# A pass width for each expert, and in the last stage a PSUM bank for the exponential with another order on ScalarE

## The chip, the cores and the metric

The kernel runs on one core of one Trainium2 chip. The metric is the device time of one launch in microseconds (us). A core has TensorE (PE, with its weight loads shown apart as PEld), VectorE (DVE), ScalarE (ACT), GpSimd (POOL) and SyncE (SP, which here only issues DMAs). Each engine works through its own instructions in the order in which they stand, and waits at an instruction until what it needs is there.

## The reference

Three parts follow each other. The first is attention with a window of 32 and 32 global positions (4 batches, 8 heads, 544 positions). The second routes each of the 2176 rows of the first to one of 8 experts. The third is a feed-forward layer with a rational function.

```python
# part 2, for each expert e (x: 2176 x 512, w1[e]: 512 x 1024, w2[e]: 1024 x 512)
mask = e_idx == e                      # e_idx = argmax(x @ w_gate)
h = np.maximum(x[mask] @ w1[e], 0.0)
out[mask] = gate_w[mask, None] * eom[mask, e, None] * (h @ w2[e])

# part 3 (w_in: 512 x 2048, w_out: 2048 x 512)
h = x @ w_in
P = a[0] + a[1] * h + a[2] * h * h + a[3] * h * h * h
Q = 1.0 + np.abs(b[0]) * np.abs(h) + np.abs(b[1]) * h * h
y = (P / (Q + 1e-06)) @ w_out
```

How many rows an expert gets depends on the data. The inputs are drawn with a fixed seed; the reference's own router gives on them, for experts 0 to 7, the counts 422, 331, 253, 249, 220, 149, 434 and 118.

## The kernel before, in words

Matrices are kept as a pair of a rounded high part and a low part, and each product is made of three matmuls (high by high, high by low, low by high), so the instruction counts are three times what one would expect.

**Experts.** Tokens are gathered by expert into an `x` tile (`xs` for expert 0, then `xa` and `x2c` in turn), columns being tokens. `wide` (line 898) is the pass without a branch: it works on the first 256 columns of an expert (`BASE`), and for expert 0 on the first 296 (`FIRST`). It takes 8 steps of 12 matmuls for the first product (line 914, into `ph`) and, two steps behind (`LAG`), 8 steps of 12 matmuls for the second (line 926, into four accumulators `acc`): 192 matmuls whose width is the number of columns. Between them ACT makes the high part of the hidden layer (`hT`, line 919) and DVE the low part (line 920). The `hT` tiles are used in turn: five of them at 256 columns, four at 296.

Tokens beyond the pass are handled in blocks of 128 columns by `single` (line 852), each behind a branch on the expert's count, in `beyond` (line 1014): the outer branch is `cnt > 256` (line 1022), the inner one `cnt > 384` (line 1024). `single` has 24 matmuls of 512 columns (line 872), transposes (lines 860 and 891) and 48 matmuls of 256 columns (line 882), and POOL stores its result (line 846). The blocks of expert e run inside the pass of expert e+1, after that one's first step (`AFTER`); while they run, the background work of the pass (weights split into high and low parts, lines 693 and 697, gathers, loads of `x`) stands still. Expert 6's columns 256 to 511 are prepared ahead, in expert 5's pass (`READY`).

**Last stage** (`moe2`, line 1213). 17 blocks of 128 tokens in five chunks of 4, 3, 4, 3 and 3 blocks (`CH`), each of 16 steps, so steps 0 to 79. In a step PE makes `h` (line 1162, 12 matmuls, 512 or 384 columns wide), the elementwise chain makes the rational function in high and low parts `gh` and `gl`, and PE multiplies these with `w_out` (line 1305, 3 matmuls of 512 columns for each block of the chunk). From step 48 on the second product runs four steps behind the first (`SK + 1`), and `gh` and `gl` have four places each, all in one tile. The elementwise chain of a step (`elem`, line 1255) in its order on each engine:

- ACT: `ab` (1265), `u` (1266), `q` (1267), then `gh` of the step before (1279), the logarithm `r0` (1282), the exponential `r` (1284)
- POOL: `q` times `ab` (1268), which needs ACT's `q`; the logarithm needs its result
- DVE: two operations on `u` (1271, 1272), `gl` of the step before (1280), then after the exponential `q` (1288), `r` (1291), `u` (1295); the next step's `gh` needs that last `u`

In chunk 0 the exponential is written to a PSUM bank (`bank_r`), in the others in place in SBUF (`r0`). In `last` (line 1327) the final three steps' second products are made block by block, and each block is copied out of PSUM (1335, 1337, 1338) and scattered to its rows by POOL (1314).

Of the kernel before, what the change touches and what calls it, by code (L numbers as in the profile page):

```python
# [24 lines left out]
E = 8  # L25
# [12 lines left out]
ACT_EXP_LN = 6  # L38
STEP = 6
NB = 2  # L40
BASE, MOST, FIRST, LAG = 256, 512, 296, 2
NX, HINT = 4, 8
READY, LATER = (6,), (5, 7)
SA, S0, S1 = "v", "a", "a"


# [21 lines left out]
TR = (1, 1), (2, 2)  # L68
HB = 4
AY = 14, 11, 2  # L70
LASTS = 3
LEAD = 2
YQ = lambda nc: nc.scalar
AQ = lambda nc: nc.gpsimd
# [27 lines left out]
class Build:  # L102
# [715 lines left out]
    def experts(self, st, first, gate):  # L818
# [5 lines left out]
        self.xgs += [xg.tile([128, DM + 1], F32, name=f"xg{n}") for n in range(2, NX)]  # L824
        for x in self.xgs[2:]:
            nc.gpsimd.memset(x, 0.0)
        yt = P("yp").tile([128, 4, FIRST], F32, name="yt")
        hp = P("hp")
        PP = lambda name, bufs: st.enter_context(tc.tile_pool(name=name, bufs=bufs, space=PSUM))
        ps_h = self.ps_h = self.ctx.enter_context(tc.tile_pool(name="ps_h", bufs=2, space=PSUM))  # L830
# [3 lines left out]
        ps_t = lambda: pools[next(turn) % len(pools)]  # L834
        col = lambda e, j: self.idx[:, NBLK * e + j:NBLK * e + j + 1]
        X = lambda e: self.xs if e == 0 else self.xa if e % 2 else self.x2c
        hT = [hp.tile([128, 2, FIRST if n < 4 else BASE], F32R, name=f"hT{n}") for n in range(NH)]
        hr = [hp.tile([128, 512], F32, name=f"hr{n}") for n in range(2)]
        PAIRS = ((0, 0), (0, 1), (1, 0))

        ORDER = [(k, 0, b) for k in range(4) for b in range(2)] + [(k, 1, 0) for k in range(4)]
        off = [0]

        def store(e, j, n, y, q):

            q.dma_start(out=self.ybuf[:, :, bass.ds(off[e] + 128 * j, n)], in_=y)

        def store_rest(y):

            nc.sync.dma_start(out=self.ybuf[:, :, FIRST:FIRST + 128], in_=y)  # L850

        def single(e, j, x, at=0, put=None, W=None, parts=2):

            W = W or self.slot[e % 2]
            hk = lambda a, k: hT[AFTER + k // 2][:, a, 128 * (k % 2):128 * (k % 2) + 128]

            def transp(n):
                pt = ps_t().tile([128, 4, 128], F32, tag="pt", name="pt")
                for c in range(4):
                    nc.tensor.transpose(pt[:, c], hr[n][:, 128 * c:128 * c + 128], self.ident)  # L860
                for a in range(2):
                    o = [hT[AFTER + 2 * n + a][:, i, 0:256] for i in range(2)]
                    self.split_t(*o, pt[:, 2 * a:2 * a + 2].rearrange("p c t -> p (c t)"))

            def hook(n, k):
                if (n, k) in TR:
                    transp(n - 1)

            for n in range(2):
                ph = ps_a.tile([128, 512], F32, tag=f"acc{n + 1}", name=f"acc{n + 1}")  # L870
                for i, (k, a, b) in enumerate(ORDER):
                    nc.tensor.matmul(ph, lhsT=x[:, a, k, at:at + 128], rhs=W[:, b, 2 * k + n, :], start=(i == 0), stop=(i == 11))
                    if i % 3 == 2:
                        hook(n, i // 3)
                nc.scalar.activation(hr[n], ph, AF.Relu)
            w = 512 // parts
            py = [ps_a.tile([128, 512], F32, tag=f"acc{m}", name=f"acc{m}")[:, 0:w] for m in (0, 3)[:parts]]
            for ks in [(k,) for k in range(6)] + [(6, 7)]:
                for m in range(parts):
                    for k in ks:  # L880
                        for i, (a, b) in enumerate(PAIRS):
                            nc.tensor.matmul(py[m], lhsT=hk(a, k), rhs=W[:, b, 8 + k, w * m:w * m + w],
                                             start=(k == 0 and i == 0), stop=(k == 7 and i == 2))
                for k in ks:
                    hook(2, k)
            y, yc = hr[0], hr[1].rearrange("p (c t) -> p c t", c=4)
            nc.scalar.copy(y[:, :256], py[0][:, 0:256])
            nc.vector.tensor_copy(y[:, 256:], py[-1][:, w - 256:w])
            pt = ps_t().tile([128, 4, 128], F32, tag="pt", name="pt")
            for c in range(4):  # L890
                nc.tensor.transpose(pt[:, c], y[:, 128 * c:128 * c + 128], self.ident)
            nc.scalar.copy(yc, pt)
            put(yc) if put else store(e, j, 128, yc, AQ(nc))

        def mark(label, hint):
            tc.mark_branch_hint_location(label, hint, [mybir.EngineType.PE])

        def wide(e, j, n, x, bg, last=True, acc=None, before=None):

            W = self.slot[e % 2]  # L900
            nh = NH if n <= BASE else 4
            rest, bg = bg, iter(()) if before else bg
            acc = [ps_a.tile([128, 512], F32, tag=f"acc{m}", name=f"acc{m}") for m in range(4)] if acc is None else acc
            for s in range(8 + LAG):
                if s == HINT and e:
                    mark(f"rest{e}", cnt[e] > BASE)
                if s == AFTER and before:
                    before()
                    bg = rest
                if s < 8:  # L910
                    ph = ps_h.tile([128, 512], F32, tag="ph", name="ph")[:, :n]
                    c = 128 * (s % 4)
                    for i, (k, a, b) in enumerate(ORDER):
                        nc.tensor.matmul(ph, lhsT=W[:, b, 2 * k + s // 4, c:c + 128], rhs=x[:, a, k, :n],
                                         start=(i == 0), stop=(i == 11))
                        if i % 6 == 5:
                            next(bg, None)
                    hi, lo = (hT[s % nh][:, a, :n] for a in range(2))
                    nc.scalar.activation(hi, ph, AF.Relu)
                    nc.vector.scalar_tensor_tensor(out=lo, in0=ph, scalar=0.0, in1=hi.bitcast(F32),  # L920
                                                   op0=ALU.max, op1=ALU.subtract)
                if s >= LAG:
                    f = s - LAG
                    for m in range(4):
                        for i, (a, b) in enumerate(PAIRS):
                            nc.tensor.matmul(acc[m][:, :n], lhsT=W[:, b, 8 + f, 128 * m:128 * m + 128],  # L926
                                             rhs=hT[f % nh][:, a, :n], start=(f == 0 and i == 0), stop=(f == 7 and i == 2))
                        if m % 2:
                            next(bg, None)
            def end():  # L930
                for m in range(4):
# [1 line left out]
                k = min(NBLK, 128 - NBLK * e)  # L933
                YQ(nc).dma_start(out=self.toks[bass.ds(off[e], 128 * k), :].rearrange("(j p) o -> j (p o)", p=128),
                                 in_=self.idxT[NBLK * e:NBLK * e + k])
                store(e, j, n, yt[:, :, :n], YQ(nc))

            if last:
                end()
# [47 lines left out]
        def more(e, j, end):  # L987

            with tc.For_i(j, end, 1) as i:
                tok = self.ixo[:, 1:2].bitcast(F32)  # L990
                nc.gpsimd.tensor_copy(tok, self.idx[:, bass.ds(i + NBLK * e, 1)])
                self.prep(NX - 1, X(e), ps_t(), 0, after=lambda: fetch(e, i + 1))
                single(e, i, X(e))
                AQ(nc).dma_start(out=self.toks[bass.ds(off[e] + 128 * i, 128), :], in_=tok,
                                 allow_slow_non_contiguous=True)

# [10 lines left out]
        def expert(e, early=lambda: ()):  # L1007

            plan = PLANW if e < E - 1 else PLANW7
            more_ = blocks(e + 1 if e + 1 in READY else e, (2, 3)) if e + 1 in READY or e not in READY + LATER else []  # L1010
            wide(e, 0, BASE, X(e), weave(todo(e, plan, None, blocks(e + 1, (0, 1)) + more_, more_ + blocks(e + 2, (0, 1))),
                                         iter(early())), before=(lambda: beyond(e - 1)) if e > 1 else second)

        def beyond(e):
            def rest_block(b, parts):
                if e in LATER:
                    self.gather(b, col(e, b))
                    self.scale(b, 128, S1)
                if e not in READY:
                    self.prep(b, X(e), ps_t(), 128 * b, scale=False, parts=2)  # L1020
                single(e, b, X(e), 128 * b, parts=parts)
            with tc.If(cnt[e] > BASE, label=f"rest{e}"):  # L1022
                rest_block(2, 2)
                with tc.If(cnt[e] > BASE + 128):
                    rest_block(3, 2 if e in READY else 1)

        def reload(e):

# [35 lines left out]


        acc = [ps_a.tile([128, 512], F32, tag=f"acc{m}", name=f"acc{m}") for m in range(4)]
        wide(0, 0, FIRST, self.xs, woven(), False, acc)()
        gate.close()
        pools.append(PP("ps_t2", 1))
        self.conv_init(P("cv"))  # L1070
# [3 lines left out]
        def second():  # L1074
# [5 lines left out]
            j0, end0 = (nc.s_assert_within(x, 0, NBLK) for x in (j0, end0))  # L1080
            self.conv_first()
            with tc.If(more0 > 0):
                single(0, 2, self.xs, put=store_rest)
            with tc.If(again0 > 0):
                fetch(0, j0)
                more(0, j0, end0)
# [126 lines left out]
    def moe2(self):  # L1213
        nc, tc, out = self.nc, self.tc, self.t["out"]
        with ExitStack() as st:
# [26 lines left out]
            load_y = lambda ch, i: self.load_y(chunks[ch][0] + i)  # L1242
            prep = lambda ch, i: self.x2_prep(chunks[ch][0] + i, x2[ch], i, nc.gpsimd if ch == 1 else nc.vector)
            steps = [(c, f) for c in range(len(chunks)) for f in range(16)]
            hs, gs, us, accs, out_, rows = {}, {}, {}, {}, [], []
            n_steps = len(steps)

            def gemm1(s):
# [6 lines left out]
            def elem(s):  # L1255
# [5 lines left out]
                if s < n_steps:  # L1261
# [1 line left out]
                    h = hs.pop(s)[:, :w]  # L1263
                    ab, q, u, r0 = (et[t_][s % len(et[t_])][:, :w] for t_ in ("ab", "q", "u", "r0"))
                    nc.scalar.activation(ab, h, AF.Abs)  # L1265
                    nc.scalar.activation(u, h, AF.Identity, scale=a3, bias=a2)  # L1266
                    nc.scalar.activation(q, ab, AF.Identity, scale=b1, bias=b0)  # L1267
                    nc.gpsimd.tensor_tensor(out=q, in0=q, in1=ab, op=ALU.mult)  # L1268
                    if rows:
                        rows.pop(0)()  # L1270
# [9 lines left out]
                    GL(nc, s - 1).tensor_tensor(out=g[1], in0=up, in1=g[0].bitcast(F32), op=ALU.subtract)  # L1280
                if s < n_steps:
                    nc.scalar.activation(r0, q, AF.Ln, bias=eps1)  # L1282
                    r = bank_r[:, :w] if first_ch(s) else r0
                    nc.scalar.activation(r, r0, AF.Exp, scale=-1.0)  # L1284
                if out_:
                    store(out_.pop())
# [193 lines left out]
```

## Time and profile before

| | |
|---|---|
| median of 3 runs | 797.82 us (796.57 to 799.12) |
| the profiled execution | 796.99 us, its span 795.4 us |
| PE, PEld busy share | 97%, 83% |
| DVE, ACT, POOL busy share | 73%, 67%, 46% |
| granted TensorE clock, mean | 0.997 of full speed |

The span is the time from the first to the last instruction; 1.6 us of the run lie around it. A busy share is an average over stages. PE's time is modelled from the starts of its matmuls, which overlap, so the time of a group is best read from start to start of the groups around it.

### The profile page before, as it was taken

To read this page: it belongs to the slowest core of one execution; us is meant where nothing else is said; L and a number is where in the kernel's file an instruction comes from. 1 tells how busy PE (TensorE), PEld (TensorE's weight loads), DVE (VectorE), ACT (ScalarE), POOL (GpSimd) and SP (SyncE) were. 2 spreads that over 40 slices of the span, in tenths; PEclk is the share of its full clock that TensorE was granted. 3 is DMA by queue.
4 is the path that set the end of the run, shared out by engine and by line. 5 is a ranking of instruction groups with operands and counts; after the bars stand their busy time and mean duration, and the time that the engine had idled before them with its cause. 6 is when DMAs were issued, how large, how long until landed. Compare 5 with 4: busy or idle time off the path is not lost. (4 is left out here: it accounts for less than half of the span.)

```text
span 795.4 us, 17092 instructions
## 1 busy us (share of the span) xinstructions
PE 769.5 (97%) x6144; PEld 661.9 (83%) x6145; DVE 579.6 (73%) x1426; ACT 536.7 (67%) x1206; POOL 366.5 (46%) x415
## 2 busy tenths in 40 slices
PE   8999998899999999999999999999999999999995
PEld 5767666798989999998988888888888898988983
DVE  5669788662828877771369999888888768888883
ACT  4667675563646766652668888878877767877772
POOL 4445555363617667540565877432252214323422
PEclk9999999999999999999999999999999999999998
DMA  8998993465748989892263440010010000000101
GB/s 296 306 314 283 278 304 106 138 190 191 269 137 269 323 292 339 302 310 71 94 185 111 120 108 25 28 54 27 0 55 14 0 1 28 27 0 1 41 1 40
DMA packets 52701, 112.88 MB, mean 142 GB/s; under 512 B 10786, under 2 KB 24866, under 8 KB 50552
## 3 DMA queue, kind: packets, MB, share of 16 engines
q1 hardware_dynamic: 42232, 96.39, 37.6%
q0 software_dynamic: 3888, 9.80, 3.9%
q10 hardware_dynamic: 6480, 5.39, 2.1%
q8 instruction: 57, 0.93, 0.5%
q14 instruction: 44, 0.36, 0.2%
HBM read 95.42 MB, written 19.03 MB: 144 GB/s over the span
## 5 line engine op out<-in xcount | busy, mean ns | idle before, releaser
L1268 POOL TENSOR_TENSOR q<-q,ab 128x384 f32<-128x384 f32 (+1 forms) x78 | 97.9, 1255 | 209.6 <-ACT q L1267 201.4
L1305 PE MATMUL acc<-slot,gh 128*128 128x512 f32 x528 | 165.8, 395 | 1.5 <-ACT gh L1279 1.5
L697 POOL TENSOR_TENSOR slot<-raw,slot 128x512 fp32r<-128x512 f32 x84 | 112.9, 1353 | 69.4 <-ACT slot L693 65.9
L1162 PE MATMUL ph<-x2c,slot 128*128 128x512 f32 (+1 forms) x552 | 125.1, 374 | 0.9 <-PEq L1022 0.4
L1162 PEld LDWEIGHTS ph<-x2c,slot 128*128 128x128 f32 x552 | 101.1, 187 | 19.6 <-ACTq L1134 0.7
L1305 PEld LDWEIGHTS acc<-slot,gh 128*128 128x128 f32 x528 | 98.3, 187 | 21.8 <-ACT gh L1279 1.9
L1305 PE MATMUL acc<-slot,gl 128*128 128x512 f32 x264 | 104.4, 395 | 0.0
L926 PE MATMUL acc<-hT,slot 128*128 128x256 f32 (+1 forms) x768 | 102.8, 284 | 0.0
L926 PEld LDWEIGHTS acc<-hT,slot 128*128 128x128 f32 x768 | 96.2, 189 | 0.2
L693 ACT CAST slot<-raw 128x512 fp32r<-128x512 f32 x144 | 85.4, 619 | 9.4 <-DVE yt L932 4.9
L314 POOL TENSOR_SCALAR pr<-ex,r 128x128 f32<-128x128 f32 x128 | 46.6, 376 | 57.0 <-PE sc L261 17.6
L1162 PE MATMUL ph<-xa,slot 128*128 128x384 f32 x384 | 71.8, 336 | 0.0
L1282 ACT ACTIVATE r<-q,cab 128x384 f32<-128x384 f32 (+1 forms) x78 | 51.4, 658 | 28.6 <-POOL q L1268 27.5
L1162 PEld LDWEIGHTS ph<-xa,slot 128*128 128x128 f32 x384 | 67.9, 188 | 2.7
L1288 DVE SCALAR_TENSOR_TENSOR q<-q,r 128x384 f32<-128x384 f32 (+1 forms) x64 | 38.6, 603 | 40.1 <-ACT r L1284 40.1
L1279 ACT CAST gh<-u 128x384 fp32r<-128x384 f32 (+1 forms) x78 | 43.4, 556 | 33.4 <-DVE u L1295 20.1
L697 DVE TENSOR_TENSOR slot<-raw,slot 128x512 fp32r<-128x512 f32 x60 | 50.4, 841 | 17.4 <-ACT slot L693 16.9
L296 ACT ACTIVATE ex<-sm,mx 128x128 f32<-128x128 f32 x128 | 50.3, 395 | 15.9 <-POOL pr L314 8.5
L1266 ACT ACTIVATE u<-ph,cab 128x384 f32<-128x384 f32 (+1 forms) x78 | 55.3, 708 | 7.1 <-POOL gl L1280 6.1
L1305 PEld LDWEIGHTS acc<-slot,gl 128*128 128x128 f32 x264 | 49.4, 187 | 12.3 <-DVE gl L1280 0.3
L1267 ACT ACTIVATE q<-ab,cab 128x384 f32<-128x384 f32 (+1 forms) x78 | 58.1, 745 | 0.0
L1272 DVE SCALAR_TENSOR_TENSOR u<-u,cab,ph 128x384 f32<-128x384 f32 (+1 forms) x78 | 51.9, 666 | 2.8
(232 smaller groups left out, 1486.4 us busy)
## 6 DMA issues: line engine op xcount, KB each, us to landing
raw<-in_w_dram SPq DMA_DIRECT2D x78, 512.0 KB
vw<-in_vw_dram SPq DMA_DIRECT2D x16, 1024.0 KB
r<-in_w_dram SPq DMA_DIRECT2D x18, 512.0 KB
kw<-in_kw_dram SPq DMA_DIRECT2D x16, 384.0 KB
raw<-wf SPq DMA_DIRECT2D x9, 512.0 KB
qt<-in_qT_dram SPq DMA_DIRECT2D x32, 128.0 KB
xbuf<-xrow SPq DMA_DIRECT2D x8, 512.0 KB
ybuf<-yt ACTq DMA_DIRECT2D x7, 512.0 KB
```

The source lines that it names most:

```text
L296: nc.scalar.activation(ex[:, h], src[:, h], AF.Exp, bias=mx[:, h:h + 1], scale=-1.0, accum_out=ssum[:, h:h + 1])
L314: nc.gpsimd.tensor_scalar(out=pr[:, h], in0=ex[:, h], scalar1=r[:, h:h + 1], scalar2=1.0, op0=ALU.mult, op1=ALU.mult)
L693: nc.scalar.copy(hi, r)
L697: eng.tensor_tensor(out=lo[:, c], in0=r[:, c], in1=hi[:, c].bitcast(F32), op=ALU.subtract)
L926: nc.tensor.matmul(acc[m][:, :n], lhsT=W[:, b, 8 + f, 128 * m:128 * m + 128], rhs=hT[f % nh][:, a, :n], start=(f == 0 and i == 0), stop=(f ...
L1162: self.nc.tensor.matmul(ph[:, :w], lhsT=l[a], rhs=r[b], start=(k == 0 and i == 0), stop=(k == 3 and i == 2))
L1266: nc.scalar.activation(u, h, AF.Identity, scale=a3, bias=a2)
L1267: nc.scalar.activation(q, ab, AF.Identity, scale=b1, bias=b0)
L1268: nc.gpsimd.tensor_tensor(out=q, in0=q, in1=ab, op=ALU.mult)
L1272: nc.vector.scalar_tensor_tensor(out=u, in0=u, scalar=a1, in1=h, op0=ALU.add, op1=ALU.mult)
L1282: nc.scalar.activation(r0, q, AF.Ln, bias=eps1)
L1305: nc.tensor.matmul(accs[i], lhsT=l[a], rhs=Wo[:, b, f, :], start=(f == 0 and j == 0), stop=(f == 15 and j == 2))
```

## The change

1. A table `WIDE` gives the width of the pass: 296 columns for expert 0, as before, and 308 for expert 6, the seventh; all others keep 256. Every place that assumed 256 now takes the expert's own width: the branches of `beyond`, the prefetch hint (line 906), the position of the blocks and of their stores. Expert 6's blocks so begin at columns 308 and 436, its branches are `cnt > 308` and `cnt > 436`. The `x` tile ends at column 512, so the second block would read from column 384 and store its last 76 columns.
2. The five `hT` tiles become two: one for the first place, as wide as the widest pass, and one that is cut into the other places by the pass's width. At 308 columns four places are used in turn.
3. From step 54 of the last stage on (`SPARE`) ACT makes `q` ahead of `u`, and the exponential and what follows from it (lines 1284 to 1295) go to the PSUM bank of the fourth accumulator, which the last two chunks, three blocks wide, don't use.

```diff
-BASE, MOST, FIRST, LAG = 256, 512, 296, 2
+BASE, MOST, LAG = 256, 512, 2
-READY, LATER = (6,), (5, 7)
+READY, LATER, WIDE = (6,), (5, 7), {0: 296, 6: 308}
+FIRST = WIDE[0]
-LASTS = 3
+LASTS, SPARE = 3, 54
...
-        yt = P("yp").tile([128, 4, FIRST], F32, name="yt")
+        wd = lambda e: WIDE.get(e, BASE)
+        widest = max(wd(e) for e in range(E))
+        yt = P("yp").tile([128, 4, widest], F32, name="yt")
...
-        hT = [hp.tile([128, 2, FIRST if n < 4 else BASE], F32R, name=f"hT{n}") for n in range(NH)]
+        h0, hs = (hp.tile([128, 2 * w], F32R, name=f"hT{n}") for n, w in enumerate((widest, (NH - 1) * BASE)))
+        hT = lambda k, n: (hs[:, 2 * n * (k - 1):2 * n * k] if k else h0[:, 0:2 * n]).rearrange("p (a t) -> p a t", a=2)
...
-            nh = NH if n <= BASE else 4
+            nh = min(NH, 1 + (NH - 1) * BASE // n)
...
-                    mark(f"rest{e}", cnt[e] > BASE)
+                    mark(f"rest{e}", cnt[e] > n)
...
-            wide(e, 0, BASE, X(e), weave(todo(e, plan, None, blocks(e + 1, (0, 1)) + more_, more_ + blocks(e + 2, (0, 1))),
+            wide(e, wd(e), X(e), weave(todo(e, plan, None, blocks(e + 1, (0, 1)) + more_, more_ + blocks(e + 2, (0, 1))),
...
         def beyond(e):
-            def rest_block(b, parts):
-                if e in LATER:
-                    self.gather(b, col(e, b))
-                    self.scale(b, 128, S1)
-                if e not in READY:
+            def rest_block(c, parts):
+                at = min(c, MOST - 128)
+                for b in range(-(-c // 128), (at + 127) // 128 + 1) if e not in READY else ():
+                    if e in LATER:
+                        self.gather(b, col(e, b))
+                        self.scale(b, 128, S1)
                     self.prep(b, X(e), ps_t(), 128 * b, scale=False, parts=2)
-                single(e, b, X(e), 128 * b, parts=parts)
-            with tc.If(cnt[e] > BASE, label=f"rest{e}"):
-                rest_block(2, 2)
-                with tc.If(cnt[e] > BASE + 128):
-                    rest_block(3, 2 if e in READY else 1)
+                single(e, c, X(e), at, parts=parts, skip=c - at)
+            n = wd(e)
+            with tc.If(cnt[e] > n, label=f"rest{e}"):
+                rest_block(n, 2)
+                with tc.If(cnt[e] > n + 128):
+                    rest_block(n + 128, 2 if e in READY else 1)
...
-                    nc.scalar.activation(u, h, AF.Identity, scale=a3, bias=a2)
-                    nc.scalar.activation(q, ab, AF.Identity, scale=b1, bias=b0)
+                    for o_, x_, k1, k0 in ((q, ab, b1, b0), (u, h, a3, a2))[::1 if s >= SPARE else -1]:
+                        nc.scalar.activation(o_, x_, AF.Identity, scale=k1, bias=k0)
...
-                    r = bank_r[:, :w] if first_ch(s) else r0
+                    if s == SPARE:
+                        spare.append(ps_a.tile([128, 512], F32, tag="acc3", name="acc3"))
+                    r = bank_r[:, :w] if first_ch(s) else spare[0][:, :w] if spare else r0
```

On PE, at the end of expert 6's pass, where expert 7's first step and the branch to expert 6's blocks follow, the kernel before has this (`slot_81` holds expert 6's weights, `slot_3338` expert 7's; `acc`, `hT` and `ph` are as above):

```order
L926 MATMUL acc_6653<-hT_3368,slot_81 128x256 x3
L926 MATMUL acc_6654<-hT_3368,slot_81 128x256 x3
L914 MATMUL ph<-xa,slot_3338 128x256 x12
L1022 COMPARE_AND_BRANCH
L872 MATMUL acc_7186<-slot_81,x2c 128x512 x12
```

At the same place the changed kernel has this:

```order
L930 MATMUL acc_6650<-hT_3367,slot_81 128x308 x3
L930 MATMUL acc_6651<-hT_3367,slot_81 128x308 x3
L918 MATMUL ph<-xa,slot_3338 128x256 x12
L1028 COMPARE_AND_BRANCH
L876 MATMUL acc_7183<-slot_81,x2c 128x512 x12
```

Only the width of expert 6's matmuls differs, 308 in place of 256. Their number and place are the same, expert 7's step keeps 256, and both blocks still stand in the program, behind their branches.

On ACT, near the end of the last stage, one step of the kernel before (`q` is written at line 1267, the logarithm at 1282, the exponential at 1284):

```order
L1265 ACTIVATE ab_8285<-ph 128x384
L1266 ACTIVATE u_8288<-ph,cab 128x384
L1267 ACTIVATE q_8286<-ab_8285,cab 128x384
L1279 CAST gh<-u_8289 128x384
L1282 ACTIVATE r_8290<-q_8286,cab 128x384
L1284 ACTIVATE r_8290<-r_8290 128x384
```

The same step in the changed kernel (both `u` and `q` are now of line 1273):

```order
L1271 ACTIVATE ab_8282<-ph 128x384
L1273 ACTIVATE q_8283<-ab_8282,cab 128x384
L1273 ACTIVATE u_8285<-ph,cab 128x384
L1285 CAST gh<-u_8286 128x384
L1288 ACTIVATE r_8287<-q_8283,cab 128x384
L1292 ACTIVATE acc_10362<-r_8287 128x384
```

`q` has moved ahead of `u`, and the exponential goes from the logarithm's SBUF tile to the PSUM bank `acc_10362`. The cast to `gh` keeps its place ahead of the logarithm.

## Rows read from the trace of the kernel before

**Rows 1.** The page, busy time and share of the span by engine.
```profile
PE 769.5 (97%) x6144; PEld 661.9 (83%) x6145; DVE 579.6 (73%) x1426; ACT 536.7 (67%) x1206; POOL 366.5 (46%) x415
```

**Rows 2.** Chain of work that ended last, its end: start us, length us, engine, work.
```profile
727.35 2.09 PE ph L1162 x12
729.44 2.12 PE acc L1305 x9
...
732.56 0.56 ACT u L1266
...
776.40 0.56 ACT u L1266
...
782.59 5.30 PE acc L1305 x21
```

**Rows 3.** Timeline, steps 78 and 79: start us, length us, engine, line, tiles, [idle before].
```profile
769.06 2.26 PE L1162 MATMUL ph<-x2c,slot 128*128 128x384 f32 x12
...
775.93 0.47 ACT L1265 ACTIVATE ab<-ph 128x384 f32<-128x384 f32 x1
...
776.30 0.67 ACT L1266 ACTIVATE u<-ph,cab 128x384 f32<-128x384 f32 x1
...
776.86 0.71 ACT L1267 ACTIVATE q<-ab,cab 128x384 f32<-128x384 f32 x1
...
777.64 1.18 POOL L1268 TENSOR_TENSOR q<-q,ab 128x384 f32<-128x384 f32 x1 [2.82 <-ACT q L1267]
...
778.85 0.62 ACT L1282 ACTIVATE r<-q,cab 128x384 f32<-128x384 f32 x1 [0.31 <-POOL q L1268]
...
779.50 0.53 ACT L1284 ACTIVATE r<-r 128x384 f32<-128x384 f32 x1
...
780.72 0.40 PE L1305 MATMUL acc<-slot,gl 128*128 128x512 f32 x1
...
782.03 0.51 ACT L1279 CAST gh<-u 128x384 fp32r<-128x384 f32 x1 [2.00 <-DVE u L1295]
782.57 0.56 DVE L1280 TENSOR_TENSOR gl<-u,gh 128x384 fp32r<-128x384 f32 x1 [0.63 <-ACT gh L1279]
...
782.59 0.73 PE L1305 MATMUL acc<-slot,gh 128*128 128x512 f32 x2 [1.47 <-ACT gh L1279]
```

**Rows 4.** Timeline of PE, expert 6's two blocks.
```profile
355.95 4.29 PE L872 MATMUL acc<-slot,x2c 128*128 128x512 f32 x18
...
368.93 0.44 PE L891 MATMUL pt<-ident,hr 128*128 128x128 f32 x2 [0.27 <-DVE hr L888]
369.12 4.38 PE L872 MATMUL acc<-slot,x2c 128*128 128x512 f32 x18
...
382.42 3.13 PE L914 MATMUL ph<-xa,slot 128*128 128x256 f32 x24
```

**Rows 5.** Timeline of PE, after expert 1's only block.
```profile
234.19 0.44 PE L891 MATMUL pt<-ident,hr 128*128 128x128 f32 x2 [0.27 <-DVEq L1024]
235.06 3.00 PE L914 MATMUL ph<-x2c,slot 128*128 128x256 f32 x24 [0.42 <-PEq L1024]
```

**Rows 6.** Busy time by engine, 370 to 380 us: length; PE, PEld, DVE, ACT, POOL; clock, DMA.
```profile
370.00:380.00 10.00, 10.00 (x66) 8.91 (x65) 1.70 (x4) 2.73 (x7) 0.81 (x1) 1.00 0.09 27
```

**Rows 7.** Timeline of PE in expert 6's pass, 256 columns.
```profile
340.60 1.53 PE L914 MATMUL ph<-x2c,slot 128*128 128x256 f32 x12
...
343.38 1.55 PE L914 MATMUL ph<-x2c,slot 128*128 128x256 f32 x12
```

**Rows 8.** Timeline of PE in expert 0's pass, 296 columns.
```profile
155.58 1.81 PE L926 MATMUL acc<-hT,slot 128*128 128x296 f32 x12
...
160.49 1.80 PE L914 MATMUL ph<-xs,slot 128*128 128x296 f32 x12
```

**Rows 9.** Groups by line, chunk 0 (414 to 490 us): xcount, busy us, mean ns.
```profile
L1295 DVE SCALAR_TENSOR_TENSOR u<-u,cab,ph 128x512 f32<-128x512 f32 x13 | 9.6, 739 | 0.0
```

**Rows 10.** The same line in chunk 2 (570 to 645 us).
```profile
L1295 DVE SCALAR_TENSOR_TENSOR u<-u,cab,r 128x512 f32<-128x512 f32 x15 | 11.3, 752 | 0.5
```

More of the change, by code (lines that the diff above doesn't have):

```diff
@@ L842, in experts, with store, single @@
         off = [0]
-        def store(e, j, n, y, q):
-            q.dma_start(out=self.ybuf[:, :, bass.ds(off[e] + 128 * j, n)], in_=y)
+        def store(e, c, n, y, q):
+            q.dma_start(out=self.ybuf[:, :, bass.ds(off[e] + c, n)], in_=y)
         def store_rest(y):
             nc.sync.dma_start(out=self.ybuf[:, :, FIRST:FIRST + 128], in_=y)
-        def single(e, j, x, at=0, put=None, W=None, parts=2):
+        def single(e, to, x, at=0, put=None, W=None, parts=2, skip=0):
             W = W or self.slot[e % 2]
-            hk = lambda a, k: hT[AFTER + k // 2][:, a, 128 * (k % 2):128 * (k % 2) + 128]
+            hk = lambda a, k: hT(AFTER + k // 2, BASE)[:, a, 128 * (k % 2):128 * (k % 2) + 128]
             def transp(n):
@@ L861, in transp @@
                 for a in range(2):
-                    o = [hT[AFTER + 2 * n + a][:, i, 0:256] for i in range(2)]
+                    o = [hT(AFTER + 2 * n + a, BASE)[:, i] for i in range(2)]
                     self.split_t(*o, pt[:, 2 * a:2 * a + 2].rearrange("p c t -> p (c t)"))
@@ L892, in single, with wide @@
             nc.scalar.copy(yc, pt)
-            put(yc) if put else store(e, j, 128, yc, AQ(nc))
+            put(yc) if put else store(e, to, 128 - skip, yc[:, :, skip:], AQ(nc))
         def mark(label, hint):
             tc.mark_branch_hint_location(label, hint, [mybir.EngineType.PE])
-        def wide(e, j, n, x, bg, last=True, acc=None, before=None):
+        def wide(e, n, x, bg, last=True, acc=None, before=None):
             W = self.slot[e % 2]
-            nh = NH if n <= BASE else 4
+            nh = min(NH, 1 + (NH - 1) * BASE // n)
             rest, bg = bg, iter(()) if before else bg
@@ L917, in wide @@
                             next(bg, None)
-                    hi, lo = (hT[s % nh][:, a, :n] for a in range(2))
+                    hi, lo = (hT(s % nh, n)[:, a] for a in range(2))
                     nc.scalar.activation(hi, ph, AF.Relu)
@@ L926, in wide @@
                             nc.tensor.matmul(acc[m][:, :n], lhsT=W[:, b, 8 + f, 128 * m:128 * m + 128],
-                                             rhs=hT[f % nh][:, a, :n], start=(f == 0 and i == 0), stop=(f == 7 and i == 2))
+                                             rhs=hT(f % nh, n)[:, a], start=(f == 0 and i == 0), stop=(f == 7 and i == 2))
                         if m % 2:
@@ L935, in end @@
                                  in_=self.idxT[NBLK * e:NBLK * e + k])
-                store(e, j, n, yt[:, :, :n], YQ(nc))
+                store(e, 0, n, yt[:, :, :n], YQ(nc))
             if last:
@@ L992, in more @@
                 self.prep(NX - 1, X(e), ps_t(), 0, after=lambda: fetch(e, i + 1))
-                single(e, i, X(e))
+                single(e, 128 * i, X(e))
                 AQ(nc).dma_start(out=self.toks[bass.ds(off[e] + 128 * i, 128), :], in_=tok,
@@ L1066, in experts @@
         acc = [ps_a.tile([128, 512], F32, tag=f"acc{m}", name=f"acc{m}") for m in range(4)]
-        wide(0, 0, FIRST, self.xs, woven(), False, acc)()
+        wide(0, FIRST, self.xs, woven(), False, acc)()
         gate.close()
@@ L1082, in second @@
             with tc.If(more0 > 0):
-                single(0, 2, self.xs, put=store_rest)
+                single(0, 256, self.xs, put=store_rest)
             with tc.If(again0 > 0):
@@ L1244, in moe2 @@
             steps = [(c, f) for c in range(len(chunks)) for f in range(16)]
-            hs, gs, us, accs, out_, rows = {}, {}, {}, {}, [], []
+            hs, gs, us, accs, out_, rows, spare = {}, {}, {}, {}, [], [], []
             n_steps = len(steps)
```

## Prediction

> **What bounds the kernel now.** I read the page's busy shares first: PE works 97% of the span, no other engine over 83% [rows 1]. So a change counts by what it takes from PE's own time, or from the few places where PE stands still. The chain of waits says where those are. From the start of the last stage it runs through PE alone, `ph` and `acc` in turn, up to 731.56 us; from there to 782.59 us it runs through the elementwise chain of ACT, POOL and DVE, and then through PE's last 21 matmuls [rows 2]. A step there costs PE 2.1 + 2.1 = 4.2 us. The elementwise chain, from ACT's `u` at 732.56 to the `u` of eleven steps later at 776.40, takes 43.84/11 = 3.99 us a step [rows 2]: a little less than PE's 4.2, so that once it is behind it hardly catches up.
>
> The timeline shows the bill. PE finishes its last `ph` group, begun at 769.06, and has only second products left, for which it needs each step's `gh`. Its last one before the gap starts at 780.72; at 9 matmuls in 2.1 us, 0.233 us each, the next was due at 780.95. It starts at 782.59, when step 79's `gh` is there [rows 3]. That is 1.64 us. The following 21 take 5.30 us [rows 2], where 20 x 0.233 + 0.40 = 5.07 would do (the wait for `gl`): 0.23 us more. So 1.87 us of PE's time in the tail are the elementwise chain's doing.
>
> Then the experts, on PE's timeline. Expert 6 has two blocks behind branches, from 355.95 and from 369.12, and at 382.42 expert 7's pass goes on [rows 4]. A block is 13.2 to 13.3 us in which PE hardly stops.
>
> **The wider pass.** With 308 columns in the pass, a second block is needed from 437 tokens on. The reference's router gives expert 6 434, so it goes. Removed are 382.42 - 369.12 = 13.30 us of PE. What comes in its place is a branch that is now not taken. Expert 1 shows this case: its inner branch is not taken either, and from the start of the block's last transposes to the next matmul pass 235.06 - 234.19 = 0.87 us [rows 5], against 369.12 - 368.93 = 0.19 us where the branch goes on into the second block [rows 4]. So expert 7's pass would go on at 368.93 + 0.87 = 369.80 us instead of 382.42: 12.62 us less.
>
> Added are 52 columns in each of expert 6's 192 matmuls. At 256 columns, 24 of them take 343.38 - 340.60 = 2.78 us, 115.8 ns each [rows 7]. At 296, 36 take 160.49 - 155.58 = 4.91 us, 136.4 ns [rows 8]. At 384, 12 take 2.09 us, 174 ns [rows 2]. Between the last two 308 lies 12 columns above 296, at 0.43 ns a column: 141.6 ns; on from the first two, at 0.52 ns: 142.6. I take 142: 192 x 26.2 = 5.03 us more. The bounds are the rows on both sides: 136.4 ns gives 3.96 us, 174 ns gives 11.2 us.
>
> [...]
>
> What else the wider pass moves: four `hT` places in turn instead of five, where expert 0 ran at 136.4 ns with four, so no wait is added. The `hT` tiles become parts of one tile; `gh` and `gl` are already kept so, and there the chain shows PE without a gap between steps [rows 2], so parts are told apart. ACT's and DVE's work on `hT` and the store grow by a fifth, beside PE. The stores, of 308 and at the narrow end 76 columns, are read back only in the last stage. Background work of expert 7's pass has nothing to lose by the missing block, since it stands still in one: from 370 to 380 us DVE is busy 1.70, ACT 2.73, POOL 0.81 us and the DMA engines 9% [rows 6]. It begins 12.6 us sooner, with the same pace against PE as before. Should loads be late after all, the cover is that first block, 13 us.
>
> **The last stage.** `q` ahead of `u` lets ACT start `q` when `ab` is done, 775.93 + 0.47 + 0.03 (the gap between ACT's logarithm and exponential) = 776.43 instead of 776.86: 0.43 us sooner for POOL and all behind it [rows 3]. By that chain alone a step would take 3.56 us. But ACT's cast to `gh` of the step before stands ahead of the logarithm: from the exponential's end (780.03) to the start of the cast are 2.00 us of DVE, then 0.51 the cast, 0.62 the logarithm, 0.53 the exponential and 0.03 between: 3.7 us [rows 3]. That is what a step takes then, 0.3 us under the 3.99 of before. Over the eleven steps the chain gains 3.2 us on its old place; it needs 1.6.
>
> The bank adds a freedom: the logarithm no longer waits until DVE has read `r`. Its price is DVE working on PSUM. Chunk 0 does this already: the last `u` takes 739 ns there [rows 9] and 752 ns with `r` in SBUF [rows 10]. I take zero, between a gain of 0.04 us a step (three operations of 13 ns) and nothing.
>
> [...]
>
> A limit stands behind that. `gh` has four places, so step 78's cast waits for PE to finish step 74's second product: from 769.06 + 2.10 come steps 73 and 74, done about 775.5. Step 79's logarithm is queued behind this cast on ACT. Then cast, logarithm and exponential (to 777.3), 2.00 of DVE, and step 79's `gh` is there at 779.8, `gl` 0.56 later, against 780.95 and 781.4 when PE asks. One us of room: the whole 1.87 us goes, and the end, copies and POOL's scatters, follows PE as it does now.
>
> **The sum.** -12.62 + 5.03 - 1.87 = -9.46 us. Against the profiled execution's own time, 796.99 us (a span of 795.4 and 1.6 around it), that is 787.5. This execution lies 0.83 us under the median of 797.82 us, and on the median the change gives 788.4 us.
>
> **The rivals.**
> A, slower: the second block runs all the same. The count decides, at 437, and 434 is two tokens under the last that fits. The trace of before shows two blocks, so a count between 385 and 512, and cannot exclude it; for it speaks that the chip routes with its own rounding. Against it: three tokens would have to change expert. Then the wider pass costs 5.03 us and only the tail gains: 797.82 + 5.03 - 1.87 = 801.0 us.
> B: the tail gains nothing, because a step of the chain does not get under 3.84 us (3.99 less the 1.64 us over eleven steps), be it by DVE on PSUM or by a wait that none of these rows shows. Then -12.62 + 5.03: 790.2 us.
> C: the wide matmuls cost more than the line through the rows, say half-way from 142 to the upper bound, 158 ns, if ACT or DVE come late with wider `hT` in a pass that also splits weights. Then 8.1 us are added instead of 5.03: 791.4 us. Expert 0's rows, with the same four places, speak against it.
>
> **How the numbers follow.** Forecast 72%, A 4%, B 13%, C 8%; the rest, 3%, for things not seen. The forecast's own range: the lower bound of the pass (3.96) and no branch gap (-13.3 in place of -12.62) give 786.6, and the runs of before spread by 1.3 us to either side. I take 786.0 to 791.6, with B and C inside and A left out. A measurement of this kernel tells 0.3%, 2.4 us, from no change. Faster by more: all but A and the unseen, 94%. Within: 2%. Slower: 4%.
>
> **What would show it.** Right: on PE only one block of expert 6, expert 7's pass going on some 13.9 us after that block's start; expert 6's groups of 12 starting 1.70 us apart instead of 1.39; POOL's `q` starting 1.3 us after ACT's `ab` instead of 1.7; PE without a gap between 771 us's counterpart and its last matmul, and the chain of waits on PE to the end. Wrong: two blocks (A); the gap before the last 21 matmuls still there (B); groups of 1.9 us (C); new gaps on PE in expert 7's pass, which would say that loads or splits had needed the second block's time.

## The result, and the profile after

| | before | after |
|---|---|---|
| median | 797.2 us (795.76 to 799.12, 4 runs) | 786.17 us (785.25 to 786.76, 4 runs) |
| profiled execution | 796.99 us, span 795.4 | 786.76 us, span 785.2 |

The ratio is 0.9863, with a 95% interval of 0.984 to 0.9885. Between the two profiled executions lie 10.2 us of span, at a granted clock of 0.997 in both. In one session below, one execution of the kernel with 436 columns (994.53 us, granted clock 0.69) and one of the kernel before (1057.34 us, 0.66) were slow; its medians and ratio leave them out.

PE's share stays 97% [rows 1], of a shorter span. The page, busy time by engine:

```profile
PE 761.8 (97%) x6060; PEld 655.4 (83%) x6061; DVE 586.3 (75%) x1421; ACT 535.0 (68%) x1198; POOL 360.7 (46%) x414
```

The timeline of PE through expert 6's pass and its block (start us, length us, engine, line, tiles, idle before and its end):

```profile
330.31 5.65 PE L918 MATMUL ph<-x2c,slot 128*128 128x308 f32 x36
335.80 1.87 PE L930 MATMUL acc<-hT,slot 128*128 128x308 f32 x12
...
345.21 1.87 PE L918 MATMUL ph<-x2c,slot 128*128 128x308 f32 x12
346.91 1.87 PE L930 MATMUL acc<-hT,slot 128*128 128x308 f32 x12
348.62 1.87 PE L918 MATMUL ph<-x2c,slot 128*128 128x308 f32 x12
...
358.81 1.60 PE L918 MATMUL ph<-xa,slot 128*128 128x256 f32 x12
360.25 4.25 PE L876 MATMUL acc<-slot,x2c 128*128 128x512 f32 x18
...
373.21 0.44 PE L895 MATMUL pt<-ident,hr 128*128 128x128 f32 x2 [0.27 <-DVEq L1030]
374.08 3.13 PE L918 MATMUL ph<-xa,slot 128*128 128x256 f32 x24 [0.43 <-PEq L1030]
```

Of the two blocks [rows 4] one is left, and expert 7's pass goes on 374.08 - 360.25 = 13.83 us after that block's start, with the 0.43 us gap of a branch not taken that expert 1 showed [rows 5]. Two groups of 12 take 348.62 - 345.21 = 3.41 us: 142.1 ns a matmul.

The end of the chain of waits (start us, length us, engine, work) is PE alone, where before the elementwise chain had stood [rows 2]:

```profile
758.67 2.10 PE acc L1313 x9
760.77 2.10 PE ph L1168 x12
762.87 14.90 PE acc L1313 x63
777.76 0.02 issue
```

Where the 10.2 us are, by PE's marks in the two traces:

| stretch, us | before | after | difference |
|---|---|---|---|
| up to expert 6's pass | 330.38 | 330.31 | -0.07 |
| the pass, to expert 7's first matmul | 24.14 | 28.50 | +4.36 |
| from there to where expert 7's pass goes on | 27.90 | 15.27 | -12.63 |
| the rest of that pass | 27.62 | 27.61 | -0.01 |
| last stage, to the start of the last 21 matmuls | 372.55 | 370.82 | -1.73 |
| from there to the end of the span | 12.81 | 12.69 | -0.12 |

### The profile page after: what moved, and what is told of

Read it like the earlier page. It is cut to its first block, busy times and chain, and to the rows that moved or that the text cites. A ratio compares the mean times of both kernels' runs of the same rounds, so it can differ in the third digit from the quotient of the medians.

```text
span 785.2 us, 16906 instructions
## 1 busy us (share of the span) xinstructions
PE 761.8 (97%) x6060; PEld 655.4 (83%) x6061; DVE 586.3 (75%) x1421; ACT 535.0 (68%) x1198; POOL 360.7 (46%) x414
## 5 line engine op out<-in xcount | busy, mean ns | idle before, releaser
L1274 POOL TENSOR_TENSOR q<-q,ab 128x384 f32<-128x384 f32 (+1 forms) x78 | 93.7, 1202 | 212.0 <-ACT q L1273 204.4
L930 PE MATMUL acc<-hT,slot 128*128 128x256 f32 (+2 forms) x768 | 105.3, 287 | 0.0
L930 PEld LDWEIGHTS acc<-hT,slot 128*128 128x128 f32 x768 | 98.5, 188 | 0.2
L923 ACT ACTIVATE hT<-ph 128x256 fp32r<-128x256 f32 (+2 forms) x64 | 25.1, 393 | 42.1 <-PE ph L918 31.5
```

## The experiments

The medians below stand beside runs of the kernel before on the same chip: 796.1 us in the session of the first four, 797.14, 796.12 and 796.63 us for the three after it.

**The wide pass alone.** The last stage is as before: `u` first, the exponential in SBUF.

```diff
-LASTS, SPARE = 3, 54
+LASTS, SPARE = 3, 99
```

> The wider pass alone; the last stage as before. If the three terms add up as they stand in the two traces (pass +4.4, block -12.6, tail -1.85 us), this is 8.3 us faster than before, about 789 us, and the gap of 1.6 us on PE before the last 21 matmuls is still there. If the wider pass had helped the tail or the other way round, the gain is nearer 10 us or the gap is smaller. Expert 6's pass from its first to expert 7's first matmul: 28.5 us if the wide matmuls leave one small gap on PE behind the branch that isn't taken (0.4 us), 29.1 if the gaps of before (0.9 us in all) come back.

Measured: 787.74 us, ratio 0.9896 (0.9876 to 0.9915), a span of 786.4. The gap of the tail is there, in PE's timeline:

```profile
771.75 0.40 PE L1313 MATMUL acc<-slot,gl 128*128 128x512 f32 x1
773.64 0.73 PE L1313 MATMUL acc<-slot,gh 128*128 128x512 f32 x2 [1.49 <-ACT gh L1285]
```

So -12.63 + 4.36 = -8.27 us of the change are the pass's: 796.1 - 787.74 = 8.4.

**The last stage alone.** Expert 6 has its 256 columns and both blocks.

```diff
-READY, LATER, WIDE = (6,), (5, 7), {0: 296, 6: 308}
+READY, LATER, WIDE = (6,), (5, 7), {0: 296}
```

> The last stage's change alone, with the shared hT tile; expert 6 keeps 256 columns and its two blocks. By the same sum 1.85 us faster than before, about 795.3 us, with the last 21 matmuls following without a gap. Expert 6's pass: 24.1 us with gaps of 0.3 and 0.45 us on PE if those belong to the narrow matmuls, which leave PE less queued work while the branch is resolved; 23.7 us if the 0.45 us gap was chance. If parts of the one hT tile were held for each other, all passes would be longer by some us.

Measured: 795.23 us, ratio 0.999 (0.9974 to 1.0005). The medians cannot tell it from no change, and say 0.9 us where the trace says more: a span of 793.2 against 795.4, and PE without a gap (780.14, then 780.37 us). So the tail's 1.85 us are shown by the traces alone. The medians of the two halves add up to 9.2 us, where the whole change gave 11.0 in its first session and 9.0 in its last.

**The order alone.** `q` goes ahead of `u`, the exponential stays in SBUF; the pass is wide.

```diff
-                    if s == SPARE:
+                    if s == 99:
...
-                    r = bank_r[:, :w] if first_ch(s) else spare[0][:, :w] if spare else r0
+                    r = bank_r[:, :w] if first_ch(s) else r0
```

> Wider pass, and q ahead of u, but the exponential stays in SBUF. Two theories of the tail. The prediction's: the chain catches up over eleven steps and needs under 3.84 us a step; here about 3.7, so there is no gap before the last 21 matmuls. The other: the chain is held at the cast of step 77, which waits for its place in gh until PE has done step 73, and only two rounds of the chain lie behind that; a round here is 3.57 to 3.65 us, so the gap is 0.1 to 0.2 us. POOL's q: 1.18 us a step if its slower half came from DVE reading two SBUF operands beside it, 1.02 if the order alone did it.

Measured: 796.45 us in one execution, 10 us above the changed kernel; neither theory had that. The order's own cost is read against the wide pass alone, from which this kernel differs by the order only: spans of 794.9 and 786.4, 8.5 us. The timeline of POOL, DVE and ACT in a step of it:

```profile
744.60 0.65 ACT L1273 ACTIVATE u<-ph,cab 128x384 f32<-128x384 f32 x1
...
744.77 1.02 POOL L1274 TENSOR_TENSOR q<-q,ab 128x384 f32<-128x384 f32 x1 [3.30 <-ACT q L1273]
...
744.87 1.33 DVE L1303 SCALAR_TENSOR_TENSOR u<-u,cab,r 128x384 f32<-128x384 f32 x1
```

DVE's last product takes 1.33 us there. The groups by line say that it does so on average, 700 to 780 us (xcount, busy us, mean ns); first this kernel, then the changed one:

```profile
L1303 DVE SCALAR_TENSOR_TENSOR u<-u,cab,r 128x384 f32<-128x384 f32 x19 | 23.9, 1258 | 0.7
```

```profile
L1303 DVE SCALAR_TENSOR_TENSOR u<-u,cab,acc 128x384 f32<-128x384 f32 x18 | 11.1, 615 | 0.6
L1274 POOL TENSOR_TENSOR q<-q,ab 128x384 f32<-128x384 f32 x17 | 17.3, 1017 | 48.3 <-ACT q L1273 48.3
```

POOL's product had begun 0.10 us before DVE's. In the kernel before it is the other way round: DVE begins, and POOL's product takes longer (timeline):

```profile
757.32 0.62 DVE L1295 SCALAR_TENSOR_TENSOR u<-u,cab,r 128x384 f32<-128x384 f32 x1
...
757.63 1.18 POOL L1268 TENSOR_TENSOR q<-q,ab 128x384 f32<-128x384 f32 x1 [2.82 <-ACT q L1267]
```

The chain of waits of the order alone runs through logarithm, exponential and DVE's three products at one round in 749.17 - 744.87 = 4.30 us, more than PE's 4.2:

```profile
744.87 1.34 DVE u L1303
746.80 0.53 ACT r L1288
747.36 0.54 ACT r L1292
747.99 0.57 DVE q L1296
748.58 0.57 DVE r L1299
749.17 1.35 DVE u L1303
```

PE falls behind and loses time at three places. First its pauses, in the timeline; then the busy times in windows, where the third figure from a row's end is the granted clock:

```profile
726.74 0.73 PE L1313 MATMUL acc<-slot,gh 128*128 128x512 f32 x2 [1.37 <-ACT raw L1332]
...
777.00 0.83 PE L1313 MATMUL acc<-slot,gh 128*128 128x512 f32 x2 [2.79 <-ACT gh L1285]
...
780.59 1.22 PE L1313 MATMUL acc<-slot,gh 128*128 128x512 f32 x2 [1.81 <-ACT gh L1285]
```

```profile
777.00:780.50 3.50, 1.62 (x3) 0.58 (x3) 2.66 (x5) 1.47 (x3) 0.00 (x0) 0.57 0.00 0
780.50:784.50 4.00, 3.91 (x10) 3.13 (x11) 0.56 (x1) 0.62 (x2) 0.86 (x1) 0.52 0.00 0
```

The first is where a chunk ends and ACT copies the accumulators out. In the windows behind the other two the granted clock was 0.57 and 0.52, and the last 21 matmuls took 6.87 us, where those of the changed kernel take 762.87 + 14.90 - 772.51 = 5.26. By PE's marks this is the whole 9.7 us by which the span is longer than the changed kernel's: 1.82 us up to 749.87 us (748.05 there), 6.26 more up to the last 21 matmuls, and 1.61 in these.

**The bank alone.** `u` first, the exponential in the free PSUM bank; the pass is wide.

```diff
-                    for o_, x_, k1, k0 in ((q, ab, b1, b0), (u, h, a3, a2))[::1 if s >= SPARE else -1]:
+                    for o_, x_, k1, k0 in ((q, ab, b1, b0), (u, h, a3, a2))[::-1]:
```

> Wider pass, and the exponential in the PSUM bank, but u ahead of q as before. POOL's q falls from 1.18 to 1.02 us if r in SBUF was what slowed it, and a step of the chain from 3.99 to about 3.8 us. By the prediction's theory (eleven steps to catch up, 3.84 needed) there is then just no gap before the last 21 matmuls. By the other (held at the cast of step 77, then two rounds) step 79's gh is late by two rounds' excess and the gap is 0.3 to 0.5 us. If POOL stays at 1.18 us the gap is over 1 us by both.

Measured: 786.03 us in one execution, a span of 784.5. Of the gap 0.23 us are left: PE's last matmul before it ends at 771.51 by the spacing, the next starts at 771.74. That lies between the two theories, no gap and 0.3 to 0.5 us. Timeline:

```profile
766.98 1.02 POOL L1274 TENSOR_TENSOR q<-q,ab 128x384 f32<-128x384 f32 x1 [3.18 <-ACT q L1273]
...
767.34 0.51 ACT L1285 CAST gh<-u 128x384 fp32r<-128x384 f32 x1 [0.43 <-DVE u L1303]
...
771.18 0.51 ACT L1285 CAST gh<-u 128x384 fp32r<-128x384 f32 x1 [2.00 <-DVE u L1303]
```

With one operand of DVE's last product in PSUM, POOL's product takes 1.02 us in this order too, not 1.18. The bank brings nearly all of the tail's gain; the order on top of it shortens the last round, 771.18 - 767.34 = 3.84 us here and 3.56 in the changed kernel. The round before it is 3.56 us here too, from 763.78.

**Another operand in PSUM.** Is it the two operands from SBUF, or the wait for `r` that comes back with the exponential in SBUF? Here `q` goes first, `r` is in SBUF, and the bank holds `u` between DVE's second and last product.

```diff
...
+                    p = spare[0][:, :w] if spare else u
-nc.vector.scalar_tensor_tensor(out=u, in0=u, scalar=a1, in1=h, op0=ALU.add, op1=ALU.mult)
+nc.vector.scalar_tensor_tensor(out=p, in0=u, scalar=a1, in1=h, op0=ALU.add, op1=ALU.mult)
...
-                    r = bank_r[:, :w] if first_ch(s) else spare[0][:, :w] if spare else r0
+                    r = bank_r[:, :w] if first_ch(s) else r0
...
-nc.vector.scalar_tensor_tensor(out=u, in0=u, scalar=a0, in1=r, op0=ALU.add, op1=ALU.mult)
+nc.vector.scalar_tensor_tensor(out=u, in0=p, scalar=a0, in1=r, op0=ALU.add, op1=ALU.mult)
```

> The changed kernel with the order q ahead of u, and the exponential in SBUF as before (as in the run of the order alone, 796.45 us), but the free PSUM bank holds the polynomial u between VectorE's second and last product instead of r. So VectorE's last product reads one operand from PSUM and one from SBUF, and the logarithm still waits until VectorE has read r. Theory 1 (VectorE's last product, with both operands in SBUF, shares its way to SBUF with GpSimd's q, and one waits for the other): the last product goes from 1.35 us back to about 0.75, a step to PE's 4.2, and the time is 786 to 787 us, a gap of at most 0.4 us before the last 21 matmuls. Theory 2 (the logarithm that waits for r makes the step long when q is early): the step stays at 4.3 us and the time at 794 to 797 us.

Measured: 785.52 us, ratio 0.9858 (0.9831 to 0.9884), as the changed kernel. In its timeline the two products start as close together as in the order alone, and neither is longer for it:

```profile
745.43 1.02 POOL L1274 TENSOR_TENSOR q<-q,ab 128x384 f32<-128x384 f32 x1 [2.85 <-ACT q L1273]
...
745.53 0.62 DVE L1304 SCALAR_TENSOR_TENSOR u<-acc,cab,r 128x384 f32<-128x384 f32 x1
```

So it is the two operands from SBUF: the logarithm waits for `r` here as in the order alone, and the time is 10.9 us less. The traces also show who pays: 0.62 becomes 1.33 us where POOL is first, 1.02 becomes 1.18 where DVE is. The second product loses 0.71 and 0.16 us, less than the 0.92 and 0.31 us that the first still had to run.

**No block at all: 436 columns.** The changed kernel with 6: 436 in `WIDE`; the inner branch and its block are left out of the program for expert 6. In this first form the columns beyond 256 leave from `hr`, in stores of their own.

```diff
-READY, LATER, WIDE = (6,), (5, 7), {0: 296, 6: 308}
+READY, LATER, WIDE = (6,), (5, 7), {0: 296, 6: 436}
...
-                store(e, 0, n, yt[:, :, :n], YQ(nc))
+                for c, w, y in outs:
+                    store(e, c, w, y[:, :, :w], YQ(nc))
...
-                with tc.If(cnt[e] > n + 128):
-                    rest_block(n + 128, 2 if e in READY else 1)
+                if n + 128 < MOST:
+                    with tc.If(cnt[e] > n + 128):
+                        rest_block(n + 128, 2 if e in READY else 1)
```

> The changed kernel with 436 columns instead of 308 in expert 6's pass, so that neither of its blocks runs (434 tokens); what the pass has beyond 256 columns is copied and stored from the two tiles that the blocks use otherwise, in 128 columns at most each. Theory 1 (the price goes by columns, and expert 7's background work needs neither block as a cover): 12 matmuls of 384 columns take 2.09 us, 174 ns each, and of 512 columns 0.233 us each; between them 436 is at 198 ns, against 142.1 measured at 308: 192 x 56 = 10.7 us more. The block that is left takes 374.08 - 360.25 = 13.83 us in the changed kernel; a branch not taken in its place 0.4 to 0.6. That is 2.6 us less than the changed kernel: 783.6 us, 782.5 to 785.0. Theory 2 (the block that is left was a cover: loads or splits for the last stage come late without it): PE stands still in expert 7's pass by several us, and the time is 786 us or more, up to 797 if the whole block is given back.

Measured: 797.49 us, ratio 1.0012 (0.9996 to 1.0028): by the number, the second theory. The timeline points elsewhere. Behind expert 0's pass, where expert 0's block begins, on ACT; then behind expert 6's pass, on ACT and PE:

```profile
187.15 0.60 ACT L879 ACTIVATE hr<-acc 128x512 f32<-128x512 f32 x1 [5.39 <-DMA ybuf<-hr]
...
377.63 2.95 ACTq L850 DMA_DIRECT2D ybuf<-hr  x2
380.92 0.62 ACT L694 CAST slot<-raw 128x512 fp32r<-128x512 f32 x1 [6.96 <-DMA ybuf<-hr]
...
382.65 2.93 PE L918 MATMUL ph<-xa,slot 128*128 128x256 f32 x12 [5.55 <-DVEq L1032]
```

Behind expert 6's pass ACT, which issues the stores, did no other work for 6.96 us, the issuing of the stores included, and the profile names those from `hr` as what it waited for; PE stood still for 5.55 us. Expert 0's result also has columns beyond 256. There ACT's write of the block's `hr` waited for the store from it, with 5.39 us of no work before it, and PE waited 2.71 us for ACT. So the edit seems to have brought a cost of its own, which the next run tests.

**436 columns, one store.** `hr` and `yt` are one tile, and the result leaves from its end in one DMA.

```diff
+        hy = P("yp").tile([128, 1024 + 4 * BASE], F32, name="yt")
+        ytail = lambda n: hy[:, 1024 + 4 * (BASE - n):].rearrange("p (m t) -> p m t", m=4)
+        yt, hr = ytail(BASE), [hy[:, 512 * n:512 * n + 512] for n in range(2)]
...
-                store(e, 0, n, yt[:, :, :n], YQ(nc))
+                store(e, 0, n, ytail(n), YQ(nc))
```

> The changed kernel with 436 columns in expert 6's pass again, but its result leaves in one store, from one place in SBUF whose first 720 columns are the tiles of the blocks' results. In the run before, the two stores more on ACT's queue held ACT for 7 us behind the pass, and the same in expert 0's pass held PE for 2.7 us; there 192 matmuls in a pass of 39.41 us against 28.50 at 308 columns confirmed the price by columns. Theory 1 (no cover is needed): 28.50 + 10.9 - 13.83 + 0.4: 2.5 us less than the changed kernel, 783.7 us, 782.5 to 785. Theory 2 (the block that is left was a cover): PE stands still in expert 7's pass also without these stores, 786 us or more.

Measured: 784.16 us, ratio 0.9835 (0.9807 to 0.9864), a span of 782.6. The timeline of PE, then of ACT behind the store:

```profile
330.45 7.76 PE L919 MATMUL ph<-x2c,slot 128*128 128x436 f32 x36
...
355.54 2.56 PE L919 MATMUL ph<-x2c,slot 128*128 128x436 f32 x12
357.93 2.55 PE L931 MATMUL acc<-hT,slot 128*128 128x436 f32 x12
360.32 2.56 PE L919 MATMUL ph<-x2c,slot 128*128 128x436 f32 x12
...
369.86 1.58 PE L919 MATMUL ph<-xa,slot 128*128 128x256 f32 x12
371.59 3.09 PE L919 MATMUL ph<-xa,slot 128*128 128x256 f32 x24
```

```profile
371.25 0.62 ACT L694 CAST slot<-raw 128x512 fp32r<-128x512 f32 x1 [1.27 <-DVE yt L937]
```

A matmul costs (360.32 - 355.54)/24 = 199.2 ns, the pass 369.86 - 330.45 = 39.41 us. Expert 7's pass then takes 29.30 us to the last stage's first matmul at 399.16, without a gap on PE but that of a branch (371.59 - 369.86 for 12 matmuls): it needs no block as a cover. The span is 11.1 us shorter than in the first form, and the two places account for it: expert 0's block takes 13.86 us here and 18.28 there, expert 7's pass 29.30 and 36.40. Beside the pauses of 2.71 and 5.55 us that is for the most part the matmuls just behind them in the first form: six of 512 columns took 191.17 - 188.57 = 2.60 us, where expert 1's same six took 230.20 - 228.73 = 1.47, and twelve of 256 columns took 385.38 - 382.65 = 2.73 us, where a later twelve took 388.33 - 386.89 = 1.44. The granted clock there was 0.94 from 370 to 400 us, and 1.00 in the 40 us before. What in the stores holds ACT so long stays open.

**Side by side.** The changed kernel and this one again, on one chip.

> The changed kernel as it is, beside the one with 436 columns on the same chip. Both theories: about 786 us, 10 us under the kernel before.

> The kernel with 436 columns and one store once more, beside the changed kernel on the same chip. Theory 1 (192 x 56 ns of columns added, a block of 13.83 us gone, 0.4 us of a branch): 2.5 us under the changed kernel, 1.5 to 3.5. Theory 2 (the two are the same, and the 1.7 us between the medians came from the chip): within 0.8 us of it.

Measured: 787.59 us, ratio 0.9888 (0.9861 to 0.9915), and 782.94 us, ratio 0.984 (0.9815 to 0.9865). The profiled spans are 784.9 and 781.4 us. The 436 columns beat both kernels. By how much the changed one these runs don't settle: the medians here differ by 4.65 us, more than either theory gave, the spans by 3.5 here and by 2.6 in the first session of each. The traces account for 39.41 - 28.50 = 10.91 us more of expert 6's pass, and 29.30 in place of 401.69 - 358.81 = 42.88 us behind it: -2.67.

## Why the prediction was right, and where its steps were not

It gave 788.4 us and a range of 786.0 to 791.6; the time is 786.17. Its sum, made against the profiled execution, was -9.46 us, where the two profiled executions differ by 10.23; most of the 0.77 is the pass. The rest of the 2.2 us between forecast and median is no more than executions of one kernel differ by: the changed kernel's later median was 787.59 us. The lower bound, 0.17 us under the time, is tighter than the prediction's own working, 786.6 less 1.3 of spread, and its 94% for a faster kernel is one more than its list gives (72 + 13 + 8).

- **The second block**: predicted -12.62 us, measured -12.63, the branch's gap included. Rival A, by which both run, is refuted by the trace.
- **The price of a column**: 142 ns at 308 columns, measured 142.1, and 199.2 at 436, where 198 was expected from the rows at 384 and 512. Rival C is refuted.
- **The pass**: the term was mis-sized, +5.03 predicted and +4.36 measured. The price of a matmul was right; 0.55 of the 0.67 us lie behind the branch at the start of the pass, which was not counted. The first 36 matmuls take 335.80 - 330.31 = 5.49 us, 0.38 more than 36 x 0.142; before they took 335.48 - 330.38 = 5.10, 0.93 more than 36 x 0.1158. The other 156 matmuls, with their transposes, have 0.84 and 0.98 us beside their price. The weight loads show the pauses, first before, then after:

```profile
332.05 1.60 PEld L914 LDWEIGHTS ph<-x2c,slot 128*128 128x128 f32 x13 [0.32 <-issue]
334.10 1.34 PEld L914 LDWEIGHTS ph<-x2c,slot 128*128 128x128 f32 x11 [0.45 <-issue]
```

```profile
332.27 3.44 PEld L918 LDWEIGHTS ph<-x2c,slot 128*128 128x128 f32 x24 [0.37 <-issue]
```

  Two pauses in which loads were not issued have become one. The lengths of the pass repeat: 24.14 and 24.22 us in the two traces at 256 columns, 28.50 to 28.51 in four at 308. Why loads are issued late there, and why a wider pass has one pause less, stays open.
- **Background work of expert 7's pass**: predicted to need no cover beyond the first block; it needs none at all, as 436 columns show.
- **The tail**: predicted -1.87 us, measured -1.73 - 0.12 = -1.85. PE runs without a gap to its last matmul, so rival B is refuted, though the order alone would have gone worse than B. That the number fits so well is in part luck: the reasons were wrong in two places.
- *What the order and the bank are worth.* The step said that `q` ahead of `u` gains 0.43 us a step and that the bank's price and gain are about zero. POOL's `q` does start 759.16 - 757.87 = 1.29 us after ACT's `ab`, as it said. But alone, the order costs 8.5 us and the bank nearly removes the gap. The step looked at POOL's start and not at what DVE would be doing then: in the old order DVE's last product had begun first and POOL paid 0.16 us, in the new one POOL begins first and DVE pays 0.7. The bank takes this away for both, and only then does the order bring anything: 3.84 - 3.56 = 0.28 us, in the last round alone. The range for the bank, a gain of 0.04 us a step to none, was much too narrow at the gain's end. The hint was in the trace of before: POOL's product took 1.01 us in two of its steps and mostly 1.18. And in one of these two steps, behind the copies at a chunk's end, DVE pays already (timeline):

```profile
733.79 1.01 POOL L1268 TENSOR_TENSOR q<-q,ab 128x384 f32<-128x384 f32 x1 [4.23 <-ACT q L1267]
...
734.31 0.90 DVE L1280 TENSOR_TENSOR gl<-u,gh 128x384 fp32r<-128x384 f32 x1
```

  Here POOL began first, and DVE's `gl`, with both operands in SBUF, takes 0.90 us, where it takes 0.56 with POOL idle [rows 3].
- *The room.* Predicted was 1.1 us; it is 0.1. The timeline of ACT's casts in the changed kernel:

```profile
764.77 0.51 ACT L1285 CAST gh<-u 128x384 fp32r<-128x384 f32 x1 [0.93 <-PE acc L1313]
...
768.34 0.51 ACT L1285 CAST gh<-u 128x384 fp32r<-128x384 f32 x1 [0.28 <-DVE u L1303]
...
771.90 0.51 ACT L1285 CAST gh<-u 128x384 fp32r<-128x384 f32 x1 [2.00 <-DVE u L1303]
```

These are the casts of steps 77, 78 and 79. The prediction let step 78's wait for PE's step 74; the last one held is step 77's, which waits for PE's step 73, and from there come two rounds, 3.57 and 3.56 us. The prediction's 3.7 was a sum of lengths; the logarithm starts 0.41 us after the cast does, though that lasts 0.51, and the exponential into PSUM takes 0.50, not 0.53. The `gh` of step 79 is there at 772.41, and PE needs it at 772.27 + 0.23 = 772.50. So the two rounds may take 772.50 - 0.51 - 764.77 = 7.22 us, 3.61 each; rival B's limit of 3.84 was too loose, as the bank alone shows, which left 0.23 us at 3.56 and 3.84. At the 3.7 us a round that was predicted, 0.2 us of the gap would have been left: two errors that offset each other.

- **The price of DVE working on PSUM**: taken as zero, and none shows: from 700 to 780 us DVE's last product takes 615 ns on average with `r` in PSUM and 618 in the kernel before, with both operands in SBUF.

## What to carry to other kernels

Before an instruction is moved, look at what the other of VectorE and GpSimd does at its new time, and count their operands from SBUF: here the price, 0.7 us on a product of 0.62, fell on an instruction that the diff doesn't touch, and one operand in PSUM removed it. An instruction that takes longer in one place than its shape takes elsewhere, as 1.18 us did beside 1.01, is a hint to be followed before the sum is made. Where a wait on a buffer's place holds a chain back, find the last step that is held and count the rounds from there.

## What was not expected of the hardware

- The 0.7 us that DVE loses to a POOL product begun 0.10 us earlier, with two operands from SBUF in both: 0.62 to 1.33 us; with one of DVE's operands in PSUM it took 0.62.
- With two stores more on its queue ACT did no other work for 6.96 us, the issuing included; with one store of the 436 columns it was 1.27 us.
- After pauses of 2.79 and 1.81 us PE ran at a granted clock of 0.52, and its last 21 matmuls took 6.87 us instead of 5.26.
